# Attention feeding two mixtures of experts on one core: for pairs 13 to 23, q and k turned by 32x32 block transposes on VectorE

## The chip, the core and the metric

The kernel runs on one core of one Trainium2 chip. The metric is the device time of one execution in microseconds; three runs of the kernel before stand behind its median. A profile of one execution, taken by the hardware profiler, gives the rows shown below. Engines are PE (TensorE), DVE (VectorE), ACT (ScalarE), POOL (GpSimd) and SP (SyncE, which here only issues DMAs); PEld is TensorE's loading of weights, which overlaps its matmuls.

## What is computed

The reference, cut to what matters (all in float32; the mixtures' weights come as float64):

```python
# q, k, v: (4 batches, 12 heads, 448 rows, 64 columns)
scores = where(mask, -1e9, (1 / sqrt(64)) * q @ k.T)       # causal mask
scores = scores - max(scores, -1)
attn = exp(scores); attn = attn / (sum(attn, -1) + 1e-9)
x = (attn @ v) as (1792 tokens, 768)                        # heads side by side
h = x @ w_in                                                # w_in (768, 2048)
x = maximum(0.01 * h, h) @ w_out                            # w_out (2048, 768)
logits = x @ phi                                            # phi (768, 32): 8 experts, 4 slots each
d = softmax of logits over the tokens;  slot_input = d.T @ x
slot_out[e] = maximum(slot_input[e] @ w1[e], 0) @ w2[e]     # w1 (8, 768, 1024), w2 (8, 1024, 768)
output = (softmax of logits over the slots) @ slot_out
```

## The kernel before

**Attention.** Two heads side by side fill 128 partitions, so there are 24 pairs, six to a batch; pair n is (b, hp) = divmod(n, 6). The 448 rows are four tiles of 112 (CP). For a pair, load_qk brings q and k in with rows on partitions (tile qk, [112, 2, 512], two buffers) by four DMAs, one for q and one for k of each head; qk_stacks turns them with eight transposes on PE into PSUM tiles qkps, from which ACT casts the rounded part and DVE subtracts the remainder (tile qkt, tag qs, two buffers), so that scores are summed from parts at higher precision. The maxima of scores come from matmuls S and a custom DVE operation (junk, mxe), turned on PE (mps) and written by ACT (mr). T holds the scores less the maxima, P = exp(T) on ACT; POOL's affine_select puts zeros above the diagonal, and POOL sums P's tiles into tsum by three adds (L441, then L445 twice, over 448 and 224 elements). O = P by v, and dn, the sum by a matmul of ones with P and tsum, are on PE; rs is dn's reciprocal, O is scaled by rs and by v's scale s_v, and goes as a rounded part and a remainder to x.

**Slots.** attention_slots is a generator, three slots to an iteration n. In its second loop (n from 7 to 24, from about 104 us) slot 1 holds the last maxima of n+1, attend and inverses of n-1 and lowering of n; slot 2 T_0 and S_3; slot 3 T_1, T_2, S_0 and S_2, qk_stacks(n+2), load_qk(n+4), load_v(n+6), columns(n-1) and reduce_v(n+5). v_scale(n // 6), the scale of a batch's v, is in slot 2 of iterations 7, 13 and 19; it is a matmul v_ps on PE and five small steps on DVE that end with v_s.

**Around it.** stage() puts one slot, one unit of up(b) (18 matmuls H of w_in by x, with g = leaky relu of H on ACT and its store g_far) and steps of the weights' conversion side by side. The conversion takes raw float64 words (raw_i, raw_o) to float32: two ACT operations (cv and cs), two DVE operations on integers (L216, L217), a multiply on POOL (cv by cs), for w_in a maximum (w_am) and scale besides, and for w_out a store to wsc. One raw load waits for the last load of attention in the program, by issue_after(last_load[0]).

**Order.** All PE instructions are chained in program order (in_order), ACT's too in the later stages (fixed). DVE, POOL and SP follow a scheduler that works from priorities; attention has a raised one. Every DMA is issued by SP, in order. conv1 is the pool of the first stage (to iteration 6); gring and conv2 reuse its space tile by tile as it comes free. att, on the other side of the memory, lives to the end of attention.

Of the kernel before, what the change touches and what calls it, by code (L numbers as in the profile page):

```python
# [34 lines left out]
def tile_attn_moe_softmoe(ctx: ExitStack, tc: tile.TileContext, q, k, v, w_in, w_out, phi, w1, w2, out, dbg=None):  # L35
    nc = tc.nc
# [291 lines left out]
    def load_qk(n):  # L328
        b, hp = divmod(n, NP)
        t = att.tile([CP, 2, 2 * NI * D], F32, tag="qk", bufs=2, name=f"qk{n}")  # L330
        t = t.rearrange("p j (c x) -> p j c x", c=NI)
        for j, src in enumerate((q, k)):
            for a in range(2):
                nc.sync.dma_start(
                    t[:, j, :, D * a : D * (a + 1)], src[b, 2 * hp + a].rearrange("(c p) d -> p c d", p=CP)
                )
        qk_t[n] = t
        loaded_last()
# [25 lines left out]

    def qk_stacks(n):

        t = qk_t.pop(n)
        st = att.tile([128, 2, 2, S], F32R, tag="qs", bufs=2, name=f"qkt{n}")
# [93 lines left out]
    def inverses(n):  # L462
# [20 lines left out]
        r_t[n] = r = att.tile([128, CP], F32, tag="r", bufs=1, name=f"r{n}")  # L483
# [27 lines left out]
    NPAIR = B * NP  # L511
    onesr = att.tile([128, CP], F32R, name="onesr")
# [4 lines left out]
    for m in (0, 64):  # L517
# [3 lines left out]
    first = att.tile([128, NI, 2, 64], F32, name="first")  # L521
    nc.gpsimd.memset(first, 0.0)
    nc.gpsimd.affine_select(
        out=first, in_=first, compare_op=ALU.not_equal, fill=1.0, base=0, pattern=[[-16, NI], [-64, 2], [0, 64]],
        channel_multiplier=1,
    )
    sixteen = att.tile([128, NI, 64], F32, name="sixteen")
    nc.gpsimd.memset(sixteen, 0.0)
    for i in range(NI):
        nc.gpsimd.memset(sixteen[:, i, 16 * i : 16 * i + 16], 1.0)  # L530
# [10 lines left out]
    def attention_slots():  # L541
# [11 lines left out]
        for n in range(NP + 1):  # L553
# [27 lines left out]
            if n + NP < NPAIR:  # L581
                load_v(n + NP)
            if NP <= n + NP - 1 < NPAIR:
                reduce_v(n + NP - 1)
            yield

        for n in range(NP + 1, NPAIR + 1):
# [5 lines left out]
            if here:  # L593
                lowering(n)
            yield
# [4 lines left out]
            if n % NP == 1 and n + NP - 2 < NPAIR:  # L600
                v_scale(n // NP)
# [6 lines left out]
            if n + 2 < NPAIR:  # L608
                qk_stacks(n + 2)
                if n + 4 < NPAIR:  # L610
                    load_qk(n + 4)
            if n + NP < NPAIR:
                load_v(n + NP)
            columns(n - 1)
            if n + NP - 1 < NPAIR:
                reduce_v(n + NP - 1)
# [220 lines left out]
    if True:  # L837
        pools[0] = tc.alloc_tile_pool(name="conv1", bufs=1)
        load_qk(0)
# [265 lines left out]
VRING = 7  # L1105
# [35 lines left out]
```

## Time and profile before

| | us |
|---|---|
| median of 3 runs | 659.64 |
| lowest, highest | 658.25, 660.18 |
| the profiled execution | 656.54 |
| its span, first to last instruction | 654.8 |
| PE busy in the span | 589.6 (90%) |
| DVE busy | 366.3 (56%) |
| ACT busy | 291.1 (44%) |
| POOL busy | 235.5 (36%) |

A page of the profile has the busy time of each engine and the chain of work that ended last, followed back from the last instruction to what released it at each step. A timeline has one engine's instructions by start, with the idle time before each and, behind an arrow, what ended it. A wait is put down to what came last. An engine that idles off the chain costs nothing.

### The profile page before, as it was taken

What the parts mean: (1) busy time and instruction counts of PE and PEld (TensorE: products, weight loads), DVE (VectorE), ACT (ScalarE), POOL (GpSimd) and SP (SyncE); (2) the same over time, 40 slices, a digit from 0 to 9 for tenths busy, and PEclk for the clock granted to TensorE, in tenths of its full rate; (3) what the DMA queues carried; (4) which work ended last, traced back from release to release, by engine and by line L of the source; (5) the groups of instructions that cost most, each with busy time, mean ns of one, the idle gap of its engine ahead of it and who ended that gap; (6) DMA issues with size and microseconds to landing.
All of it is one profiled execution on the core that took longest, in us unless ns stands there. A gap on an engine that the chain in (4) does not pass through costs nothing.

```text
span 654.8 us, 12495 instructions
## 1 busy us (share of the span) xinstructions
PE 589.6 (90%) x4938; PEld 341.8 (52%) x4938; DVE 366.3 (56%) x884; ACT 291.1 (44%) x571; POOL 235.5 (36%) x247
## 2 busy tenths in 40 slices
PE   3678888998999999999999999999989999998794
PEld 2455555655555565665556555554434444553454
DVE  5868658989956665747457766533674332001014
ACT  2577556678864556755546554431212111011013
POOL 5187963489584445525335532430000000000000
PEclk9999989998999999999999999999999998899997
DMA  9942336764542466553335323029967439999958
GB/s 180 283 122 50 72 75 187 212 181 135 156 134 71 132 201 193 169 158 99 83 105 135 80 68 97 29 67 334 397 238 293 162 143 381 427 419 422 425 227 336
DMA packets 102594, 125.69 MB, mean 192 GB/s; under 512 B 69256, under 2 KB 91272, under 8 KB 98440
## 3 DMA queue, kind: packets, MB, share of 16 engines
q1 hardware_dynamic: 102536, 124.89, 58.3%
q8 instruction: 39, 0.64, 0.4%
q14 instruction: 19, 0.16, 0.1%
HBM read 105.74 MB, written 19.14 MB: 191 GB/s over the span
## 4 chain that ended last, share of the span: by engine, by line
PE 62%; DMA 11%; DVE 9%; POOL 8%; ACT 5%; issue 3%; SPq 1%; ACTq 0%; POOLq 0%; DVEq 0%
PE H L102 28%; DMA w<-in_moe_w_dram 8%; PE O L102 5%; PE T L102 5%; PE g_acc L102 3%; PE S L102 3%; PE dn L102 2%; DVE g_nat L635 2%; PE qkps L102 2%; DMA raw_i_None<-in_moe_w_in_dram 2%; PE L L102 2%; PE wt_ps L102 2%; PE ph L989 2%; POOL w L245 2%; ACT P L113 2%
## 5 line engine op out<-in xcount | busy, mean ns | idle before, releaser
L102 PE MATMUL H<-x,w 128*128 128x448 f16 x1152 | 230.9, 355 | 0.7 <-ACT g L113 0.7
L102 PEld LDWEIGHTS <-w 128*128 128x128 f16 x1152 | 111.2, 99 | 111.8 <-issue 19.0
L396 DVE CUSTOM_DVE_ANT_0 junk<-S,mask 112x224 bf16<-112x224 f32 (+3 forms) x192 | 85.2, 444 | 59.9 <-PE S L102 57.0
L474 DVE RECIPROCAL rs<-rs 128x224 f32<-128x224 f32 x36 | 53.4, 1523 | 40.3 <-ACT rs L113 40.3
L113 ACT ACTIVATE P<-T 112x672 f32<-112x672 f32 (+1 forms) x72 | 57.0, 793 | 22.2 <-PE T L102 21.0
L436 POOL TENSOR_SCALAR_AFFINE_SELECT P<-P 112x448 f32<-112x448 f32 x48 | 31.0, 648 | 91.0 <-ACT P L113 53.8
L102 PE MATMUL T<-qkt 64*112 64x336 f32 (+3 forms) x576 | 60.1, 321 | 4.1 <-ACT P L113 3.3
L113 ACT ACTIVATE g<-H,iv 128x448 f32<-128x448 f32 x48 | 30.4, 634 | 66.6 <-PE H L102 47.4
L102 PE MATMUL O<-P,v 112*64 112x448 f32 (+3 forms) x384 | 52.5, 414 | 4.5 <-POOL P L436 4.4
L102 PEld LDWEIGHTS T<-qkt 64*112 64x112 f32 x576 | 42.7, 179 | 14.3 <-issue 5.7
L445 POOL TENSOR_TENSOR tsum<-tsum,P 112x448 f32<-112x448 f32 (+1 forms) x48 | 47.3, 986 | 1.9
L102 PEld LDWEIGHTS O<-P,v 112*64 112x64 f32 x384 | 25.4, 139 | 29.4 <-issue 11.9
L441 POOL TENSOR_TENSOR tsum<-P 112x672 f32<-112x672 f32 x24 | 39.1, 1629 | 1.8
L113 ACT ACTIVATE g_spare<-H,iv 128x448 f32<-128x448 f32 x16 | 10.1, 634 | 66.5 <-PE H L102 66.5
L102 PE MATMUL S<-qkt 64*112 64x224 f32 (+3 forms) x192 | 31.9, 373 | 8.5 <-DVE mxe L396 3.7
L981 POOL MEMSET hz<- 128x256 f32 x2 | 0.6, 311 | 104.1 <-PE g_acc L102 104.1
L374 DVE TENSOR_TENSOR qkt<-qkps,qkt 128x448 fp32r<-128x448 f32 x48 | 29.1, 621 | 9.8 <-ACT qkt L113 9.8
L102 PE MATMUL T<-mr,onesr 64*112 64x448 f32 (+1 forms) x192 | 30.7, 316 | 3.9 <-ACT mr L113 3.9
L236 POOL TENSOR_TENSOR cv_i_None<-cv_i_None,cs_i_None 128x768 f32<-128x768 f32 x16 | 28.6, 1786 | 12.0 <-ACT cs_i_None L113 12.0
L113 ACT ACTIVATE mr<-mps,own 128x112 fp32r<-128x112 f32 x96 | 26.2, 360 | 14.9 <-PE mps L102 14.8
L113 ACT COPY rs<-dn 128x448 f32<-128x448 f32 x18 | 9.6, 532 | 50.3 <-PE dn L102 50.3
L254 POOL TENSOR_TENSOR cv_o_None<-cv_o_None,cs_o_None 128x768 f32<-128x768 f32 x10 | 16.5, 1646 | 42.4 <-DVE cv_o_None L217 18.4
(178 smaller groups left out, 920.9 us busy)
## 6 DMA issues: line engine op xcount, KB each, us to landing
w<-in_moe_w_dram SPq DMA_DIRECT2D x31, 1536.0 KB
raw_i_None<-in_moe_w_in_dram SPq DMA_DIRECT2D x16, 768.0 KB
raw_o_None<-in_moe_w_out_dram SPq DMA_DIRECT2D x10, 768.0 KB
g_far<-g SPq DMA_DIRECT2D x32, 224.0 KB
gb<-g_far SPq DMA_DIRECT2D x8, 896.0 KB
wo<-wsc SPq DMA_DIRECT2D x4, 1536.0 KB
qk<-in_q_dram SPq DMA_DIRECT2D x48, 112.0 KB
qk<-in_k_dram SPq DMA_DIRECT2D x48, 112.0 KB
```

Source lines behind the costliest of these rows:

```text
L102: op(*args, **kwargs)
L113: op(*args, **kwargs)
L236: nc.gpsimd.tensor_tensor(t, t, sg, ALU.mult)
L245: nc.gpsimd.tensor_tensor(lo, w, hi, ALU.subtract)
L254: nc.gpsimd.tensor_tensor(wo, wo, sg, ALU.mult)
L374: nc.vector.tensor_tensor(st[:, j, 1], p, st[:, j, 0].bitcast(F32), ALU.subtract)
L396: nc.vector.tensor_tensor_reduce(out=junk[:, :w], in0=ps[:, a, at : at + w], in1=mask[:, S - w :], scale=-1.0, scalar=3e38, op0=ALU.add, o ...
L436: nc.gpsimd.affine_select(out=d, in_=d, compare_op=ALU.is_ge, fill=0.0, base=0, pattern=[[0, 4], [1, CP]], channel_multiplier=-1,)
L441: nc.gpsimd.tensor_tensor(tsum[:CP], p[0][:CP, :, 0, CP:], p[0][:CP, :, 1, : S - CP], ALU.add)
L445: nc.gpsimd.tensor_tensor(y, y, p[1][:CP, :, j, : S - CP * (j + 2)], ALU.add)
L474: nc.vector.reciprocal(rs[:, c : c + S // 2], rs[:, c : c + S // 2])
L635: nc.vector.transpose(g_nat[:, :, 32 * f : 32 * (f + n)].rearrange("p c (f x) -> p f c x", x=32), gts[b, f].rearrange("p (c x) -> p c x", ...
```

## The change

For pairs from BLOCKS = 13 on, load_qk brings each head's q and k in with eight DMAs of 32 partitions by 14 runs of 32 elements (128 bytes a run), in such a way that two 32x32 block transposes on DVE (qk_turn) give q and k with the 64 columns of two heads on the 128 partitions. The results (qx, two buffers) are in SBUF, and ACT's cast and DVE's subtract read them there; the eight PE transposes of the pair are gone. qk_turn(n+2) is in slot 1 and qk_stacks(n+2) in slot 2 for these pairs. In the second loop load_qk(n+4) stands in slot 1, and each load from pair 9 on is put right behind SP's last instruction in the program. qk tiles of the first nine pairs are in conv1, as are first, sixteen and r; qs has three buffers. load_v and reduce_v come one pair later, the ring of v has six buffers in place of seven, and v_scale is in slot 3 ahead of columns. The diff, without moves of the constants first and sixteen:

```diff
--- before.py
+++ after.py
@@ -327,13 +327,27 @@
 
     def load_qk(n):
         b, hp = divmod(n, NP)
-        t = att.tile([CP, 2, 2 * NI * D], F32, tag="qk", bufs=2, name=f"qk{n}")
+        behind = last_on(mybir.EngineType.SP) if n >= NP + 3 else None
+        if n >= BLOCKS:
+            t = att.tile([128, 2, 2 * NI * D], F32, tag="qk", bufs=2, name=f"qk{n}")[:, :, :S]
+            for j, src in enumerate((q, k)):
+                for a in range(2):
+                    rows = src[b, 2 * hp + a].rearrange("(c i) (e x) -> e i c x", i=32, x=32)
+                    for e in range(2):
+                        o = 64 * a + 32 * e
+                        with tc.issue_after(behind):
+                            nc.sync.dma_start(t[o : o + 32, j].rearrange("i (c x) -> i c x", x=32), rows[e])
+            qk_t[n] = t
+            loaded_last()
+            return
+        t = (pools[0] if n < NP + 3 else att).tile([CP, 2, 2 * NI * D], F32, tag="qk", bufs=2, name=f"qk{n}")
         t = t.rearrange("p j (c x) -> p j c x", c=NI)
         for j, src in enumerate((q, k)):
             for a in range(2):
-                nc.sync.dma_start(
-                    t[:, j, :, D * a : D * (a + 1)], src[b, 2 * hp + a].rearrange("(c p) d -> p c d", p=CP)
-                )
+                with tc.issue_after(behind) if behind is not None else ExitStack():
+                    nc.sync.dma_start(
+                        t[:, j, :, D * a : D * (a + 1)], src[b, 2 * hp + a].rearrange("(c p) d -> p c d", p=CP)
+                    )
         qk_t[n] = t
         loaded_last()
 
@@ -362,10 +376,27 @@
         nc.vector.tensor_reduce(am[:, NP:], am[:, :NP], AX.X, ALU.max)
         s_v[b], inv_v[b] = pow2_scale(am[:, NP:], f"v{b}")
 
+    turned = {}
+
+    def qk_turn(n):
+
+        if n < BLOCKS:
+            return
+        t = qk_t.pop(n)
+        turned[n] = xs = [att.tile([128, S], F32, tag="qx", bufs=2, name=f"qx{n}_{j}") for j in range(2)]
+        for j, x in enumerate(xs):
+            nc.vector.transpose(x.rearrange("p (c x) -> p c x", x=32), t[:, j].rearrange("p (c x) -> p c x", x=32))
+
     def qk_stacks(n):
 
+        st = att.tile([128, 2, 2, S], F32R, tag="qs", bufs=3, name=f"qkt{n}")
+        if n >= BLOCKS:
+            for j, x in enumerate(turned.pop(n)):
+                scalar.copy(st[:, j, 0], x)
+                nc.vector.tensor_tensor(st[:, j, 1], x, st[:, j, 0].bitcast(F32), ALU.subtract)
+            st_t[n] = st
+            return
         t = qk_t.pop(n)
-        st = att.tile([128, 2, 2, S], F32R, tag="qs", bufs=2, name=f"qkt{n}")
         for j in range(2):
             p = ps_tr(f"qkps{n}_{j}", (128, S))
             for c in range(NI):
@@ -480,7 +511,7 @@
                 mm(
                     dn[64 * a : 64 * a + 64], sixteen[:, i], x, start=i == 0, stop=i == NI - 1, skip_group_check=True,
                 )
-        r_t[n] = r = att.tile([128, CP], F32, tag="r", bufs=1, name=f"r{n}")
+        r_t[n] = r = pools[0].tile([128, CP], F32, tag="r", bufs=1, name=f"r{n}")
         nc.vector.reciprocal(r, dn)
 
     def columns(n):
@@ -509,6 +540,7 @@
         nc.gpsimd.tensor_tensor(x16[b][:, hp, 1], rs, hi, ALU.subtract)
 
     NPAIR = B * NP
+    BLOCKS = 2 * NP + 1
     onesr = att.tile([128, CP], F32R, name="onesr")
     nc.vector.tensor_copy(onesr, istack[:, 0:1].to_broadcast([128, CP]))
     nc.vector.tensor_scalar(onesr, onesr.bitcast(F32), 0.0, 1.0, ALU.mult, ALU.add)
@@ -578,10 +600,10 @@
                 qk_stacks(n + 2)
                 if n + 4 < NPAIR:
                     load_qk(n + 4)
-            if n + NP < NPAIR:
-                load_v(n + NP)
-            if NP <= n + NP - 1 < NPAIR:
-                reduce_v(n + NP - 1)
+            if n > 0:
+                load_v(n + NP - 1)
+            if n > 1:
+                reduce_v(n + NP - 2)
             yield
 
         for n in range(NP + 1, NPAIR + 1):
@@ -592,28 +614,32 @@
             inverses(n - 1)
             if here:
                 lowering(n)
+            if n + 2 < NPAIR:
+                qk_turn(n + 2)
+                if n + 4 < NPAIR:
+                    load_qk(n + 4)
             yield
             if here:
                 weights(n, 0)
             if more:
                 maxima(n + 1, TILES[0])
-            if n % NP == 1 and n + NP - 2 < NPAIR:
-                v_scale(n // NP)
+            if BLOCKS <= n + 2 < NPAIR:
+                qk_stacks(n + 2)
+            if n + NP - 2 < NPAIR:
+                reduce_v(n + NP - 2)
             yield
             if here:
                 weights(n, 1)
                 weights(n, 2)
             if more:
                 maxima(n + 1, TILES[1])
-            if n + 2 < NPAIR:
+            if n + NP - 1 < NPAIR:
+                load_v(n + NP - 1)
+            if n % NP == 1 and n + NP - 2 < NPAIR:
+                v_scale(n // NP)
+            if n + 2 < BLOCKS:
                 qk_stacks(n + 2)
-                if n + 4 < NPAIR:
-                    load_qk(n + 4)
-            if n + NP < NPAIR:
-                load_v(n + NP)
             columns(n - 1)
-            if n + NP - 1 < NPAIR:
-                reduce_v(n + NP - 1)
             yield
 
     TILES = ((3,), (0, 2), (1,))
@@ -1102,7 +1138,7 @@
 MIX = ""
 NSPARE = 6
 GAP = 5
-VRING = 7
+VRING = 6
 GAPS = (6, 15)
 
 
```

**VectorE, iterations 9 and 10** (S10 are score tiles of pair 10, qkt11 pair 11, cv_i13 a block of w_in, S11_1 the first maxima of iteration 10). Before:

```order
L396 ISA junk10_2_1_1992,mxe0_142<-S10_0_1981,mask_114 112x336
L396 ISA mxe0_142 112x1
L374 TENSOR_TENSOR qkt11_1994<-qkps11_0_1995,qkt11_1994 128x448
L374 TENSOR_TENSOR qkt11_1994<-qkps11_1_2002,qkt11_1994 128x448
L215 TENSOR_REDUCE w_am13_2022<-cv_i13_None_2023 128x1
L216 TENSOR_SCALAR cv_i13_None_2023<-cv_i13_None_2023 128x768
L217 SCALAR_TENSOR_TENSOR cv_i13_None_2023<-raw_i13_None_1694,cv_i13_None_2023 128x768
L129 TENSOR_REDUCE w12_m1_2057<-w12_ps_2055 128x1
L396 ISA junk11_1_0_2068,mxe1_143<-S11_1_2065,mask_114 112x224
```

Now:

```order
L405 TENSOR_TENSOR qkt11_2003<-qkps11_0_2004,qkt11_2003 128x448
L427 ISA junk10_2_1_1999,mxe0_131<-S10_0_1988,mask_114 112x336
L427 ISA mxe0_131 112x1
L405 TENSOR_TENSOR qkt11_2003<-qkps11_1_2011,qkt11_2003 128x448
L215 TENSOR_REDUCE w_am13_2023<-cv_i13_None_2024 128x1
L388 STREAM_TRANSPOSE qx13_0_2352<-qk13_1867 128x448
L216 TENSOR_SCALAR cv_i13_None_2024<-cv_i13_None_2024 128x768
L217 SCALAR_TENSOR_TENSOR cv_i13_None_2024<-raw_i13_None_1697,cv_i13_None_2024 128x768
L388 STREAM_TRANSPOSE qx13_1_2353<-qk13_1867 128x448
L129 TENSOR_REDUCE w12_m1_2058<-w12_ps_2056 128x1
L427 ISA junk11_1_0_2069,mxe1_132<-S11_1_2066,mask_114 112x224
```

Pair 13's two transposes have come in around the two integer steps of cv_i13, ahead of the maxima S11_1.

**GpSimd, iterations 13 and 14** (P0 and tsum are pair 14, x16 of rs13 pair 13, cv_o4 and cv_o5 blocks of w_out). Before:

```order
L436 AFFINE_SELECT P0_448_144<-P0_448_144 112x4x112
L441 TENSOR_TENSOR tsum_148<-P0_448_144 112x672
L436 AFFINE_SELECT P0_224_145<-P0_224_145 112x4x112
L445 TENSOR_TENSOR tsum_148<-tsum_148,P0_224_145 112x2x224
L509 TENSOR_TENSOR x16_2_2887<-rs13_2967,x16_2_2887 128x448
L445 TENSOR_TENSOR tsum_148<-tsum_148,P0_224_145 112x2x112
L254 TENSOR_TENSOR cv_o4_None_3156<-cv_o4_None_3156,cs_o4_None_3157 128x768
L254 TENSOR_TENSOR cv_o5_None_3271<-cv_o5_None_3271,cs_o5_None_3272 128x768
```

Now:

```order
L467 AFFINE_SELECT P0_448_133<-P0_448_133 112x4x112
L472 TENSOR_TENSOR tsum_137<-P0_448_133 112x672
L467 AFFINE_SELECT P0_224_134<-P0_224_134 112x4x112
L540 TENSOR_TENSOR x16_2_2887<-rs13_2964,x16_2_2887 128x448
L476 TENSOR_TENSOR tsum_137<-tsum_137,P0_224_134 112x2x224
L254 TENSOR_TENSOR cv_o4_None_3153<-cv_o4_None_3153,cs_o4_None_3154 128x768
L476 TENSOR_TENSOR tsum_137<-tsum_137,P0_224_134 112x2x112
L254 TENSOR_TENSOR cv_o5_None_3287<-cv_o5_None_3287,cs_o5_None_3288 128x768
```

The first of the two conversions, cv_o4, has moved from behind the last sum to ahead of it; the same stands for pairs 15 and 16.

**ScalarE, iteration 13, slot 3** (P1 is pair 13, x16 of rs12 is pair 12, which takes the new scale of v; wp_ps and wt_ps are PSUM tiles of the mixture that share two buffers with qkps and v_ps). Before:

```order
L113 ACTIVATE P1_448_146<-T13_1_2819 112x2x336
L113 ACTIVATE P1_224_147<-T13_2_2831 112x2x336
L113 CAST qkt15_2865<-qkps15_0_2866 128x448
L113 CAST qkt15_2865<-qkps15_1_2873 128x448
L113 CAST x16_2_2887<-rs12_2703 128x448
L113 ACTIVATE cv_o2_None_2894<-raw_o2_None_2171 128x768
L113 ACTIVATE cs_o2_None_2895<-raw_o2_None_2171 128x768
L113 ACTIVATE g1_2_2923<-H1_2_2904,iv1_2724 128x448
L113 COPY w4_0_2933<-wp_ps0_2926 96x128
L113 COPY wt1_2935<-wt_ps1_0_2936 128x384
L113 COPY wt1_2935<-wt_ps1_1_2941 128x384
```

Now:

```order
L113 ACTIVATE P1_448_135<-T13_1_2828 112x2x336
L113 ACTIVATE P1_224_136<-T13_2_2840 112x2x336
L113 CAST x16_2_2887<-rs12_2704 128x448
L113 ACTIVATE cv_o2_None_2891<-raw_o2_None_2182 128x768
L113 ACTIVATE cs_o2_None_2892<-raw_o2_None_2182 128x768
L113 ACTIVATE g1_2_2920<-H1_2_2901,iv1_2738 128x448
L113 COPY w4_0_2930<-wp_ps0_2923 96x128
L113 COPY wt1_2932<-wt_ps1_0_2933 128x384
L113 COPY wt1_2932<-wt_ps1_1_2938 128x384
```

The casts of qkt15 have left slot 3 (they stand a slot ahead, behind P of T13_0); x16 now follows the P of this pair. On TensorE v_ps has moved from behind S_3 in slot 2 to behind S_0 and S_2 in slot 3, where qkps was.

## Rows read from the trace of the kernel before

**Rows 1.** The page: the chain that ended last, by engine and by line.

```profile
PE 62%; DMA 11%; DVE 9%; POOL 8%; ACT 5%; issue 3%; SPq 1%; ACTq 0%; POOLq 0%; DVEq 0%
PE H L102 28%; DMA w<-in_moe_w_dram 8%; PE O L102 5%; PE T L102 5%; PE g_acc L102 3%; PE S L102 3%; PE dn L102 2%; DVE g_nat L635 2%; PE qkps L102 2%; DMA raw_i_None<-in_moe_w_in_dram 2%; PE L L102 2%; PE wt_ps L102 2%; PE ph L989 2%; POOL w L245 2%; ACT P L113 2%
```

**Rows 2.** Busy time by stretch: window, length, busy per engine, clock.

```profile
164.00:182.00 18.00, 16.86 (x124) 10.08 (x120) 17.80 (x43) 14.74 (x26) 11.11 (x9) 1.00 0.51 154
...
182.00:395.00 213.00, 207.60 (x1610) 124.39 (x1612) 132.71 (x306) 121.44 (x253) 101.17 (x93) 1.00 0.44 124
```

**Rows 3.** Waits of PE, 182 to 395 us: total, times, longest.

```profile
PE wt_ps L102 <- ACT wprime L113: 1.9, 6, 0.7
```

**Rows 4.** Pieces of the chain of waits: start, length, what.

```profile
196.18 0.92 PE qkps L102 x8
...
389.13 0.92 PE qkps L102 x8
```

**Rows 5.** By tile: durations in ns, minimum, median, maximum; first and last start.

```profile
L102 PE MATMUL qkps<-ident,qk x192: 259/259/451, 4.1 to 389.8; 112*128 112x112 f32 x192
...
L374 DVE TENSOR_TENSOR qkt<-qkps,qkt x48: 611/620/626, 5.7 to 391.2; 128x448 fp32r<-128x448 f32 x48
...
L635 DVE STREAM_TRANSPOSE g_nat<-g x16: 631/645/647, 343.3 to 445.0; 128x448 f32<-128x448 f32 x16
```

**Rows 6.** Waits of DVE, 182 to 395 us.

```profile
DVE junk L396 <- PE S L102: 44.5, 23, 6.1
```

**Rows 7.** Timelines at iterations 9 and 10: DVE, PE, SP.

```profile
161.94 2.86 DVE L216 TENSOR_SCALAR cv_i_None<-cv_i_None 128x768 int32<-128x768 int32 x1
...
166.04 0.32 PE L102 MATMUL mps<-ident,mxe 112*128 112x112 f32 x1 [0.58 <-DVE w_m L129]
...
158.41 1.03 SPq L334 DMA_DIRECT2D qk<-in_q_dram  x2
```

**Rows 8.** Timelines around tsum: POOL and PE, then DVE beside them.

```profile
257.30 1.37 POOL L445 TENSOR_TENSOR tsum<-tsum,P 112x224 f32<-112x224 f32 x1
...
260.49 0.73 PE L102 MATMUL dn<-tsum,onesr 128*64 128x336 f32 x4
...
298.69 1.37 POOL L445 TENSOR_TENSOR tsum<-tsum,P 112x224 f32<-112x224 f32 x1
...
301.25 0.73 PE L102 MATMUL dn<-tsum,onesr 128*64 128x336 f32 x4
...
415.85 0.66 POOL L445 TENSOR_TENSOR tsum<-tsum,P 112x224 f32<-112x224 f32 x1
...
416.56 0.79 PE L102 MATMUL dn<-tsum,onesr 128*64 128x336 f32 x4 [0.19 <-POOL tsum L445]
...
248.30 0.96 DVE L217 SCALAR_TENSOR_TENSOR cv_o_None<-raw_o_None,cv_o_None 128x768 int32<-128x768 int32 x1
...
256.48 1.67 DVE L217 SCALAR_TENSOR_TENSOR cv_o_None<-raw_o_None,cv_o_None 128x768 int32<-128x768 int32 x1
```

**Rows 9.** DMA packets, 197 to 200 and 25.5 to 26.5; SP's waits.

```profile
DMA packets 1387, 0.34 MB, mean 115 GB/s; under 512 B 1387, under 2 KB 1387, under 8 KB 1387
...
DMA packets 1031, 0.21 MB, mean 206 GB/s; under 512 B 1005, under 2 KB 1031, under 8 KB 1031
...
SPq L699 <- ACT g L113: 54.6, 15, 9.2
```

**Rows 10.** Timelines of iteration 13: PE, DVE, ACT.

```profile
223.96 0.49 PE L102 MATMUL v_ps<-ident,v_am 128*128 128x128 f32 x2
...
227.52 0.68 DVE L507 SCALAR_TENSOR_TENSOR rs<-O,v_s,rs 128x448 f32<-128x448 f32 x1
...
231.20 0.97 ACT L113 CAST qkt<-qkps 128x448 fp32r<-128x448 f32 x2 [0.36 <-PE qkps L102]
232.05 0.58 ACT L113 CAST x<-rs 128x448 f16<-128x448 f32 x1
```

**Rows 11.** ACT's waits, 0 to 60 us.

```profile
30.37 0.93 ACT L113 ACTIVATE cv_i_None<-raw_i_None 128x768 f32<-128x768 f32 x1 [2.95 <-DMA raw_i_None<-in_moe_w_in_dram]
```

More of the change, by code (lines that the diff above doesn't have):

```diff
@@ L520, in tile_attn_moe_softmoe @@
         )
[L521 to L530, printed above, removed]
     mxe = [att.tile([CP, 128], F32, name=f"mxe{x}") for x in range(2)]
@@ L838, in tile_attn_moe_softmoe @@
         pools[0] = tc.alloc_tile_pool(name="conv1", bufs=1)
+        first = pools[0].tile([128, NI, 2, 64], F32, name="first")
+        nc.gpsimd.memset(first, 0.0)
+        nc.gpsimd.affine_select(
+            out=first, in_=first, compare_op=ALU.not_equal, fill=1.0, base=0, pattern=[[-16, NI], [-64, 2], [0, 64]],
+            channel_multiplier=1,
+        )
+        sixteen = pools[0].tile([128, NI, 64], F32, name="sixteen")
+        nc.gpsimd.memset(sixteen, 0.0)
+        for i in range(NI):
+            nc.gpsimd.memset(sixteen[:, i, 16 * i : 16 * i + 16], 1.0)
         load_qk(0)
```

## The prediction

> **What bounds the kernel now.** First the page's engine totals (TensorE is busy in 90% of the span) and the chain that ended last [rows 1]: TensorE holds 62% of it; the transposes by matmul that the change takes away (`qkps`) hold 2%. Then busy time by stretch [rows 2]: from 182 to 395 us, where ten of the eleven changed pairs lie (the eleventh transposes at 389.1), TensorE is busy for 207.6 of 213 us at full clock, VectorE for 133. So there a microsecond off TensorE is a microsecond off the end, until another engine is late. Which one is late next is told by TensorE's waits there [rows 3]: the longest group is 1.9 us in six waits for ScalarE; none is for VectorE's maxima or GpSimd's sums. From 164 to 182 us it is otherwise: VectorE is busy for 17.8 of 18 us and is itself the chain. Near the end the load of the last weights (`w`, 8% of the span) is on the chain [rows 1]; it is released by work that the change leaves as it is, so I carry a shift at 395 us on to the end one to one.
>
> **What is taken from TensorE.** A pair's eight transposes stand on the chain as one piece of 0.92 us, between the S matmuls and the next H; there are eleven such pieces, from 196.18 to 389.13, of which the first and the last are shown [rows 4]. The single matmul shows 259 ns [rows 5], so eight would be 2.1 us; I take the chain's 0.92, since they overlap and the next H starts right after it. The order shows that only those 22 rows, of four transposes each, leave TensorE. **11 x 0.92 = 10.1 us, a gain.**
>
> **What VectorE and ScalarE get.** Two block transposes of 128x448 f32 a pair: the trace has this shape, 645 ns [rows 5]; 22 x 0.645 = 14.2 us. The two casts (0.97 us together [rows 10]) and the two subtracts (620 ns each [rows 5]) stay and move a slot ahead. From 182 to 395 us VectorE waits 44.5 us for S matmuls [rows 6], some 4 us a pair, against 1.3 us added: hidden by that wait, and 14.2 us dear if that cover were gone. ScalarE's casts stand in slot 2 behind the P of T_0, where H takes 3.41 us and the work ahead of the next g (casts 0.97, conversions 1.8) takes 2.8: hidden, with 0.6 us to spare. One thing changes in kind: the subtract read PSUM and now reads two SBUF tiles. Before, it never took over 626 ns [rows 5]; the conversion that reads two SBUF tiles (L217) took 0.96 us with GpSimd idle and 1.67 beside GpSimd's sums, which themselves took 1.37 beside it and 0.66 without [rows 8]. So a subtract can now cost 0.6 to 1.3 us. I count nothing for it, as slot 2 has VectorE's wait, but it feeds the second rival. The Trainium skill ("SBUF — State Buffer", Who interferes with whom) says that a VectorE instruction with two SBUF inputs and a GpSimd instruction that reads SBUF exclude each other through a shared port; the rows just named agree, and if all 22 subtracts doubled VectorE would get 14 us more, by that page, against none in my sum.
>
> **The first turn, iteration 10: a loss of 2.0 us (1.3 to 3.5).** The order puts pair 13's two transposes between the conversion steps of cv_i13, into the stretch where VectorE is the chain: ahead of a step of 2.86 us at 161.94, some rows before the maxima that mps reads, for which TensorE waited 0.58 us already [rows 7]. So both transposes count, 1.3 us. The load: its buffer comes free with pair 11's transposes on TensorE (158.2), and then come eight issues. Two issues took 1.03 us from 158.41 [rows 7], so four of the eight, all that the first transpose needs, are out at about 160.5. A pair's 448 KB in 256-byte packets moves at 1387 packets in some 2.6 us [rows 9], which at 128 bytes would be 3584 packets in 6.7 us at the same packet rate; the stretch that comes nearest to 128-byte packets has 1031 in a microsecond [rows 9], so 3.5 us. I take the latter, as it is the nearest in kind: half of it takes 1.75, and the last of its packets land some 2 us after the fourth issue, at 162.6, 0.7 us after the transpose's place at 161.9. 1.3 + 0.7 = 2.0; with the slower rate 3.5, with none 1.3. Later turns come nearly two iterations after their buffer is free, of 19.3 us each in the mean (389.13 - 196.18 over ten [rows 4]).
>
> **v's scale a slot later: a loss of 2.5 us (1.0 to 4.5).** In iteration 13, v_ps was on TensorE at 223.96, rs, which needs v's scale, ran from 227.52, and ScalarE's x cast of it at 232.05, late only by its place in line [rows 10]. Now v_ps stands where qkps stood (the casts of qkps began at 231.20 [rows 10]), is done at about 231.0, and its five steps lie between S_0's junks on VectorE, done at about 233.4; rs 0.68 more: 234.1. ScalarE waits there in order with x, and behind it are cv_o and cs_o (0.9 each), g and the copy of wp_ps. x 0.5, cv and cs 1.7, g 0.6, copy 0.25: 237.2. The second wt_ps on TensorE takes the PSUM buffer that this copy frees, and would be due at 235.45 - 0.92 + 0.5, near 235.0. **2.0 us (1 to 3)**. Iterations 7 and 19 have the same step with no raw_o conversion of this size behind it: 0.5 for the two (0 to 1.5).
>
> **GpSimd's order: a loss of 1.7 us (0.6 to 2.7).** For pairs 14, 15 and 16 a cv_o add of 1.65 us is put ahead of the last tsum, which dn on TensorE waits for. Before, pair 14's last tsum ended at 258.67 and dn<-tsum began at 260.49: 1.8 us to spare, of which 0.92 goes with qkps; the order takes 1.65: late by 0.7 at most, by nothing if the last tsum runs in 0.66. Pair 15 shows the same 1.8. Pair 16: end 300.06, dn 301.25, so late by 0.7 to 1.4 [rows 8]. Central values 0.4, 0.4, 0.9. For the other eight pairs the order keeps the sums together or puts in half an add. What they then do is seen in pair 23, which has no qkps ahead of it and an add of 0.92 in between: dn waited 0.19 us [rows 8]. 8 x 0.1 = **0.8 us (0 to 1.6)**.
>
> **The start: a gain of 0.5 us (-1.3 to +1.0, the gain cut to 1.0 as other waits follow).** One v load of 224 KB fewer is issued ahead of the raw weights; by the 2.6 us of 448 KB [rows 9] raw_i comes up to 1.3 us earlier, and ScalarE waited 2.95 us for one [rows 11]. Against it GpSimd's first pair has an add of 1.8 us moved ahead of its select. The later weights' buffers (raw_i6 on) now wait for pair 8's transposes on TensorE, in iteration 6; the conversions that read them are an iteration later, and I count nothing, but a late one would cost its lateness once.
>
> **Sum.** 10.1 + 0.5 - 2.0 - 2.5 - 1.7 - 0.8 = 3.6 us. The profiled run had a span of 654.8 and a time of 656.54, which becomes 652.9; the median of the runs is 3.1 us above that run, 659.64, and I predict against the median: **656.0**. With every bound at its best the gain is 8.2 (651.4), at its worst a loss of 3.5 (663.1).
>
> **Rivals.** (1) *All covers hold*: no loss at all, 659.64 - 10.1 = 649.5. For it: VectorE's 44.5 us of waiting and TensorE's few waits. Against it: iteration 10 and iteration 13 have their losers on the chain or a row behind it.
> (2) *The wait takes the place of the transposes*: dn waits for the sums in every pair. Pair 14's sums had 1.8 us to spare [rows 8], less 0.92; contention with the subtracts, or an x cast 0.9 us later, in each pair eats the rest. Then 8 x 0.7 more is lost, 3.6 - 5.6 = -2.0, which is 661.6; half of it gives 658.8, and that I take for this case: no change.
> (3) *Slower: the loads come late to an in-order VectorE.* A turn stands ahead of S_0's junks, so a late load holds the maxima, mps, mr and T. SP issues in order, and its waits for g reach 9.2 us [rows 9]; with eight issues (4.1) and 6.7 us of packets that is 20 us, a whole iteration. It decides from the point where a load lands over two iterations after its release or, for SP, where qk stands behind a g that waits in each; if six turns are late by 2 us, 3.6 - 12 = -8.4: 668; if three, 662. Against it: the loads have nearly two. The Trainium skill ("DMA: Bandwidth & Descriptors", Bandwidth, and Why small descriptors are slow (HBM only)) speaks against this edit: transfers under 64 KB are dominated by descriptors, and a load here becomes 56 KB in 128-byte runs; by its fixed cost of three cycles a packet the bytes would cost (4+3)/4 against (8+3)/8, an estimated 27% more, so some 3.3 us for the 2.6, which alone does not make this rival. No row of before has a stretch of 128-byte packets alone.
> That the edit does not do what it says is excluded: the 22 rows of four transposes are gone from TensorE's order.
>
> **How the numbers follow.** About 0.3%, 2 us, is what a measurement of this kernel can tell from no change. Forecast (a gain of 2 to 7): 0.40. Rival 1 (more than 7): 0.14. Rival 2 (within 2): 0.25. Slower, by rival 3 or by the upper bounds of my losses together: 0.21. Faster 0.54, same 0.25, slower 0.21. The range runs from 649.5 to 662: it leaves out some 0.04 below and the worse half of the slower cases, 0.11, above.
>
> **What would show it.** In the changed kernel's trace: TensorE's chain without qkps from 182 us on, S followed by H (the gain); VectorE idle ahead of the transposes of pair 13 and mps late by 2 us at about 166 (first turn); wt_ps waiting for a ScalarE copy near 235 (v's scale); dn waiting for tsum in pairs 14 to 16 and by not more than 0.2 in others (GpSimd). If dn waits by 0.5 or more in most pairs, rival 2 is right; if VectorE idles ahead of turns past pair 13, rival 3. The prediction is wrong above all if the end from 440 us on does not carry the shift.

## The result, and the profile after

The changed kernel takes 661.9 us, the median of 11 runs (659.95 to 665.99); the kernel before took 657.88 in 11 runs beside it and earlier (655.53 to 660.18). The ratio is 1.0069, with a 95% interval of 1.0046 to 1.0092: slower, by about 4 us. The profiled execution has a span of 659.1 us against 654.8. From its page, the first line and the busy time of the engines:

```profile
span 659.1 us, 12407 instructions
...
PE 586.9 (89%) x4850; PEld 334.3 (51%) x4850; DVE 369.5 (56%) x906; ACT 290.5 (44%) x571; POOL 235.0 (36%) x247
```

TensorE is busy for 2.7 us less, in a span that is 4.3 us longer. So the matmuls did go, and more than their time came back as waiting and as a lower clock. What TensorE waits for, from 100 to 400 us of the changed kernel (who waits, for what, total, times, longest; [rows 3] has the same view of the kernel before, from 182 us on):

```profile
PE dn L102 <- POOL tsum L476: 6.1, 6, 2.0
PE S L102 <- ACT P L113: 2.7, 1, 2.7
...
PE T L102 <- DVE mxe L427: 1.2, 1, 1.2
...
PE qkps L102 <- DVE v_am L369: 0.9, 1, 0.9
```

In the same window of the kernel before, the first and the last group are missing, and the one for mxe is

```profile
PE T L102 <- DVE mxe L396: 0.5, 1, 0.5
```

Where the span went is seen best by cutting it at the first matmul of O of a pair (iteration n runs from the O of pair n-1 to that of pair n; lengths in us, from the timelines of TensorE; e1 to e3 are the first three experiments below):

| stretch | before | after | e1_sums | e2_hold | e3_both |
|---|---|---|---|---|---|
| start to O of pair 6 | 104.2 | 102.0 | 107.1 | 101.7 | 102.1 |
| iteration 7 | 18.64 | 25.05 | 22.98 | 18.82 | 18.83 |
| 8 to 10 | 59.79 | 59.49 | 58.67 | 59.55 | 58.67 |
| 11 and 12 | 33.68 | 35.40 | 31.97 | 35.38 | 31.97 |
| 13 and 14 | 42.05 | 41.49 | 41.45 | 41.41 | 41.41 |
| 15 to 17 | 62.25 | 64.44 | 60.50 | 65.35 | 60.76 |
| 18 to 23 | 112.76 | 109.65 | 109.11 | 109.59 | 109.11 |
| O of pair 23 to the end | 221.4 | 221.6 | 220.1 | 219.9 | 220.8 |

Two places lose: **iteration 7**, 6.4 us, where no pair is turned yet, and **iterations 11, 12 and 15 to 17**, where the gain of the turned pairs has become a loss of 3.9. From iteration 18 on the gain is there, and the end carries the shift one to one.

**Iteration 7.** VectorE there (start, length, what, and in brackets the idle time before it and what ended it):

```profile
111.64 0.69 DVE L371 TENSOR_REDUCE v_am<-v 112x1 f32<-112x512 f32 x1 [3.13 <-DMA v<-in_v_dram]
...
115.11 0.62 DVE L427 CUSTOM_DVE_ANT_0 junk<-S,mask 112x448 bf16<-112x448 f32 x1
```

SP's issues in the same timeline, ahead of it:

```profile
100.62 1.56 SPq L183 DMA_DIRECT2D raw_i_None<-in_moe_w_in_dram  x3
104.16 0.33 SPq L357 DMA_DIRECT2D v<-in_v_dram  x1
```

VectorE stands for 3.13 us in front of the maximum of v for pair 12, the first of the third batch. With six buffers v of pair 12 has to wait for O of pair 6 (which starts at 102.02); SP issues it at 104.16, after three loads of raw weights, and it lands at about 111.6. The program writes this maximum in iteration 8, and holds each maximum behind VectorE's last instruction of the program at that point. For the first pair of a batch, though, reduce_v clears the batch's tile first, so that the last instruction is that clearing: an instruction that has nothing to wait for but the tile, and which the scheduler may put early. That of pair 12's batch ran at 18.88 us. So nothing held the maximum at its place in the program any more; the scheduler put it into iteration 7, ahead of its own data, and everything behind it on VectorE is 3 us late. The kernel before has the same hold: there the ring of seven let v of pair 12 be issued at 94.30, and the maximum ran at 130.65 without a wait. A ring of seven in the changed kernel was not tried. On TensorE:

```profile
115.79 0.57 PE L102 MATMUL T<-qkt 64*112 64x224 f32 x6 [1.20 <-DVE mxe L427]
...
118.40 1.01 PE L102 MATMUL qkps<-ident,qk 112*128 112x112 f32 x4 [0.60 <-DVE w_m L129]
120.34 1.01 PE L102 MATMUL qkps<-ident,qk 112*128 112x112 f32 x4 [0.93 <-DVE v_am L369]
121.14 5.49 PE L102 MATMUL H<-x,w 128*128 128x448 f16 x18
```

TensorE waits by pieces, 1.20, 0.60 and 0.93 us (and 0.20 for v_ps), and then its 18 matmuls H take 5.49 us where they take 3.57 in most other places. The busy time by stretch has the reason (window, length, busy per engine in the order of the page, then the granted clock, the share of the DMA engines and GB/s):

```profile
116.00:120.00 4.00, 2.60 (x26) 1.83 (x24) 3.93 (x13) 1.26 (x2) 3.83 (x4) 0.77 0.00 0
120.00:124.00 4.00, 3.66 (x12) 1.99 (x13) 3.30 (x17) 1.19 (x3) 1.06 (x3) 0.50 0.33 74
124.00:128.00 4.00, 4.00 (x21) 2.06 (x21) 1.12 (x4) 2.30 (x4) 1.01 (x1) 0.87 0.97 270
```

A granted clock of 0.50 is the lower of the two levels, 1.2 GHz. The waits cost 2.9 us, H 1.9 more, and the transposes ahead of it are slow as well.

**The sums.** GpSimd at pair 15:

```profile
283.66 1.14 POOL L476 TENSOR_TENSOR tsum<-tsum,P 112x448 f32<-112x448 f32 x1
284.75 1.64 POOL L254 TENSOR_TENSOR cv_o_None<-cv_o_None,cs_o_None 128x768 f32<-128x768 f32 x1
286.35 0.65 POOL L476 TENSOR_TENSOR tsum<-tsum,P 112x224 f32<-112x224 f32 x1
```

and TensorE beside it:

```profile
284.68 0.36 PE L102 MATMUL dn<-P,onesr 128*64 128x112 f32 x4
287.05 0.79 PE L102 MATMUL dn<-tsum,onesr 128*64 128x336 f32 x4 [2.01 <-POOL tsum L476]
...
287.92 3.57 PE L102 MATMUL H<-x,w 128*128 128x448 f16 x18
```

The conversion's product stands between the last two sums, as the order had it, and dn waits 2.01 us for the last; the granted clock stayed at 1.00 there (284 to 292 us), and the next H took 3.57. Pairs 14 and 16 wait 1.02 and 0.98. At pair 11 the remainder of w takes that place, in front of both sums; GpSimd:

```profile
204.34 1.65 POOL L245 TENSOR_TENSOR w<-cv_i_None,w 128x768 f16<-128x768 f32 x1
205.94 1.87 POOL L476 TENSOR_TENSOR tsum<-tsum,P 112x448 f32<-112x448 f32 x2
```

and TensorE:

```profile
207.86 0.79 PE L102 MATMUL dn<-tsum,onesr 128*64 128x336 f32 x4 [1.30 <-POOL tsum L476]
...
211.35 4.75 PE L102 MATMUL H<-x,w 128*128 128x448 f16 x18
```

Here H is slow again, 4.75 us, after the wait of 1.30 and one of 0.64 for mr.

### The profile page after: what moved, and what is told of

Its sections match the earlier page's. It is cut to its first block, busy times and chain, and to the rows that moved or that the text cites. A ratio compares the mean times of both kernels' runs of the same rounds, so it can differ in the third digit from the quotient of the medians.

```text
span 659.1 us, 12407 instructions
## 1 busy us (share of the span) xinstructions
PE 586.9 (89%) x4850; PEld 334.3 (51%) x4850; DVE 369.5 (56%) x906; ACT 290.5 (44%) x571; POOL 235.0 (36%) x247
## 4 chain that ended last, share of the span: by engine, by line
PE 37%; DMA 8%; DVE 4%; ACT 1%; POOL 1%; issue 0%; POOLq 0%; DVEq 0%; ACTq 0%; SPq 0%
PE H L102 18%; DMA w<-in_moe_w_dram 8%; PE g_acc L102 3%; DVE g_nat L661 2%; PE T L102 2%; PE L L102 2%; PE O L102 2%; PE ph L1025 2%; PE o L1096 1%; PE psi L997 1%; PE dn L102 1%; PE wt_ps L102 1%; PE S L102 1%; ACT P L113 1%; PE pgt L102 1%; PE lt L102 0%
## 5 line engine op out<-in xcount | busy, mean ns | idle before, releaser
L102 PE MATMUL H<-x,w 128*128 128x448 f16 x1152 | 235.7, 360 | 0.7 <-ACT g L113 0.7
L476 POOL TENSOR_TENSOR tsum<-tsum,P 112x448 f32<-112x448 f32 (+1 forms) x48 | 44.4, 924 | 1.5
L472 POOL TENSOR_TENSOR tsum<-P 112x672 f32<-112x672 f32 x24 | 40.5, 1689 | 1.7
L236 POOL TENSOR_TENSOR cv_i_None<-cv_i_None,cs_i_None 128x768 f32<-128x768 f32 x16 | 27.1, 1695 | 17.7 <-ACT cs_i_None L113 17.7
L540 POOL TENSOR_TENSOR x<-rs,x 128x448 f16<-128x448 f32 x24 | 28.8, 1199 | 10.5 <-ACT x L113 10.5
```

The lines of the kernel that those rows point to most:

```text
L102: op(*args, **kwargs)
L236: nc.gpsimd.tensor_tensor(t, t, sg, ALU.mult)
L472: nc.gpsimd.tensor_tensor(tsum[:CP], p[0][:CP, :, 0, CP:], p[0][:CP, :, 1, : S - CP], ALU.add)
L476: nc.gpsimd.tensor_tensor(y, y, p[1][:CP, :, j, : S - CP * (j + 2)], ALU.add)
L540: nc.gpsimd.tensor_tensor(x16[b][:, hp, 1], rs, hi, ALU.subtract)
```

## The experiments

Theory: two faults of order, neither of them in the turns, cost what the turns bring: (A) the maximum of v for pair 12 is ordered ahead of its data; (B) conversion work on GpSimd stands ahead of the sums that dn waits for. Rivals: the turns themselves do not pay (VectorE's added work, late loads or contention cost what TensorE saves). A third suspect is v's scale in slot 3. Four of the kernels change the order alone, four how many pairs are turned. e1_sums, e2_hold, e3_both and e4_noturn were timed beside the kernel before at 657.64 us, the others beside it at 657.34.

**e1_sums: the sums first.** In the changed kernel, GpSimd's product of cv_o and the remainder of w (the latter in the later stages only) are held behind the last add of tsum that precedes them in the program (last_sum is set behind the adds in weights):

```diff
-        nc.gpsimd.tensor_tensor(lo, w, hi, ALU.subtract)
+        with tc.issue_after(last_sum[0]) if fixed[0] and last_sum[0] is not None else ExitStack():
+            nc.gpsimd.tensor_tensor(lo, w, hi, ALU.subtract)
...
-            nc.gpsimd.tensor_tensor(wo, wo, sg, ALU.mult)
+            with tc.issue_after(last_sum[0]) if last_sum[0] is not None else ExitStack():
+                nc.gpsimd.tensor_tensor(wo, wo, sg, ALU.mult)
...
+            last_sum[0] = last_on(mybir.EngineType.Pool)
```

> The changed kernel with one thing put back: on GpSimd each conversion multiply (cv_o) and each w_in remainder is ordered behind the last tsum add of the newest pair; no other engine's order changes. Theory 1 (GpSimd's order took the place of the transposes): TensorE's waits of dn for tsum, 6.1 us in the changed kernel (1.30, 1.02, 2.01, 0.98 and two of 0.38), fall under 0.5, the H at 211 us that took 4.75 us after such a wait goes back to 3.5, and the time falls by 5 to 7 us, to 655 to 657. Theory 2 (only iteration 7 matters): the waits go, but something behind them is late by as much, and the time stays within 2 us of 661.9. Rival 3 of the prediction (late loads): no change.

Measured: 652.33 us (10 runs), ratio 0.9924 [0.9896, 0.9953]. Waits of dn for the sums fall from 6.1 to 0.5 us. In the table, iterations 11 and 12 and 15 to 17 shrink by 3.4 and 3.9 us, iterations 8 to 10 by 0.8; iteration 7 still has 4.1 more than e3_both. VectorE, ScalarE and SP run their instructions in the same order as in the changed kernel; only GpSimd's differs. So B is 9.6 us of medians (661.9 - 652.3).

**e2_hold: the maximum stays in its place.** What the maximum is held behind is looked up ahead of the clearing:

```diff
+        ahead = last_on(mybir.EngineType.DVE) if b else None
         if hp == 0:
             v_am[b] = am = const.tile([128, NP + 1], F32, tag="v_am", bufs=2, name=f"v_am{b}")
             nc.vector.memset(am, 0.0)
-        with tc.issue_after(last_on(mybir.EngineType.DVE)) if b else ExitStack():
+        with tc.issue_after(ahead) if b else ExitStack():
```

> The changed kernel with one thing put back: the first maximum of a batch's v (pairs 12 and 18) is held at its place in the program, where in the changed kernel only the clearing of its tile ahead of it was; on VectorE it moves from iteration 7 to iteration 8, nothing else does. Theory 2 (VectorE waits in order for v of pair 12, which lands behind three raw loads): VectorE's wait of 3.1 us at 108.5 goes, TensorE's waits in iteration 7 (1.2, 0.2, 0.6, 0.9) and its fall to the lower clock with them, iteration 7 falls from 25.0 us to 19 to 20, and the time by 5 to 6.5 us, to 655.5 to 657. If raw loads that come late on ScalarE, or v's scale a slot later, are the cause instead, iteration 7 stays over 23 us and the time over 660.

Measured: 654.52 us (10 runs), 0.9965 [0.9941, 0.9988]. On VectorE the maxima of pairs 6, 12 and 18, the first of their batches, move, and one step of the conversion beside that of pair 12 changes its place. Pair 6's move shows in no time: O of pair 6 starts at 101.69 us, against 102.02. Iteration 7 takes 18.82 us, about as before the change (18.64), and the waits for the sums remain (6.0 us). A is 7.4 us (661.9 - 654.5).

**e3_both: both edits.**

> Both orders put back, GpSimd's multiplies behind the sums and the first maxima of v in their place; the transposes on VectorE stay. If the two are the whole loss and add up, the time is 661.9 - 6 - 6 = 650 (648.5 to 652), about 1.2% under the kernel before. If one hides the other, or a third wait follows (wt_ps for ScalarE in iteration 13, mr for T), it stays at 653 to 656. If late loads or transposes on VectorE are the cause, over 658.

Measured: 646.06 us (4 runs, 645.04 to 649.13), 0.9843 [0.9796, 0.9891]: the fastest version, 1.6% faster than the kernel before and 2.4% faster than the change. Its page:

```profile
span 643.6 us, 12414 instructions
```

and its waits of TensorE from 100 to 400 us:

```profile
PE S L102 <- ACT P L114: 2.7, 1, 2.7
...
PE dn L102 <- POOL tsum L480: 0.5, 1, 0.5
```

The sums now come one behind the other and the product follows, as these rows of GpSimd at pair 15 show:

```profile
272.13 1.87 POOL L480 TENSOR_TENSOR tsum<-tsum,P 112x448 f32<-112x448 f32 x2
273.96 1.64 POOL L257 TENSOR_TENSOR cv_o_None<-cv_o_None,cs_o_None 128x768 f32<-128x768 f32 x1
```

In the stretch where the change lost its clock, that of e3_both stays whole (busy time by stretch):

```profile
116.00:120.00 4.00, 4.00 (x26) 2.33 (x25) 3.31 (x15) 1.64 (x4) 3.76 (x4) 1.00 0.35 79
120.00:124.00 4.00, 4.00 (x33) 2.25 (x31) 3.30 (x10) 2.57 (x5) 1.03 (x1) 1.00 1.01 291
```

A and B together are 15.8 us. They add up nearly: 7.4 and 8.5 one way (e2, then e3), 9.6 and 6.3 the other. By the ratios to the kernel before, together they are 14.9.

**e4_noturn and e5_both_noturn: no pair turned**, in the changed kernel and in e3_both. TensorE transposes all pairs again; the rest of the change (buffers of v, slots, loads in order) stays.

```diff
-    BLOCKS = 2 * NP + 1
+    BLOCKS = 4 * NP
```

> The changed kernel with TensorE's transposes for all pairs (no block transposes, loads of q and k by four DMAs, qk_stacks in slot 3 again); v later, six v buffers, the pools and load_qk in slot 1 stay. If the block transposes save what the chain said (10.1 us, of which dn's waits for the sums give back some 3.6 as each gets 0.92 more room), the time is 666 to 670. If the transposes on VectorE or their loads are what made the change slow, it is under 660.

> The kernel with both orders put back (646.06 us), but with TensorE's transposes for all pairs, as in the run without block transposes. This prices the block transposes with the two waits gone. If they are worth what the chain of waits showed, 11 x 0.92 = 10.1 us, less 1.3 for the first turn: 655 to 656. If dn's wait for the sums hides part of it even now: 650 to 653. If they are worth only the 2.6 us by which the earlier pair of runs differed (664.5 against 661.9): 648 to 649.

Measured: e4_noturn 664.48 us (4 runs), 1.0140 [1.0074, 1.0205]; e5_both_noturn 655.35 (10 runs), 0.9969 [0.9937, 1.0001]. With both orders mended the turns are worth 655.35 - 646.06 = 9.3 us (8.3 by their ratios to the kernel before). In the order of the change they are worth 664.48 - 661.9 = 2.6 (4.7 by the ratios, whose intervals overlap: from four runs of e4_noturn, this is not clear of noise). In e4_noturn dn waits for the sums, from 100 to 400 us:

```profile
PE dn L102 <- POOL tsum L476: 0.7, 2, 0.4
```

In the change it is 6.1: nearly all waits of B come with the turns. These take 0.92 us of TensorE's work from ahead of dn, and GpSimd's order is another; which of the two weighs more was not separated. The wait of iteration 7 is in e4_noturn too (25.5 us between the two O, from 102.5 to 128.0); it has nothing to do with the turns.

**e6_vslot2: v's scale back in slot 2**, in e3_both.

```diff
@@ slot 2
+            if n % NP == 1 and n + NP - 2 < NPAIR:
+                v_scale(n // NP)
@@ slot 3
-            if n % NP == 1 and n + NP - 2 < NPAIR:
-                v_scale(n // NP)
```

> The kernel with both orders put back, and v's scale in slot 2 again in place of slot 3. The prediction put the later scale at 2.5 us; the traces show one wait of 0.89 to 0.97 us of wt_ps for ScalarE in iteration 13. By the trace: that wait goes and the time is 645 (644 to 646.5). By the prediction's term: 643.5. If the scale in slot 2 holds VectorE up elsewhere: 647 or more.

Measured: 666.25 us (4 runs), 1.0106 [1.0033, 1.0178]. The expectation missed by some 20 us. The waits of TensorE from 100 to 400 us:

```profile
PE v_ps L102 <- DVE v_am L380: 14.0, 3, 5.3
```

and a piece of iteration 13, TensorE:

```profile
228.79 0.77 PE L102 MATMUL v_ps<-ident,v_am 128*128 128x128 f32 x2 [5.32 <-DVE v_am L380]
229.36 5.28 PE L102 MATMUL H<-x,w 128*128 128x448 f16 x18
```

with VectorE's last maximum of v ahead of it:

```profile
226.39 0.67 DVE L375 TENSOR_REDUCE v_am<-v 112x1 f32<-112x512 f32 x1
```

The last maximum of a batch is now made in slot 2 of the same iteration, at 226.39, since loads and maxima of v come a pair later; with the scale in slot 2, v_ps comes up on TensorE before that maximum is made and waits 4.06, 5.32 and 4.60 us, and H after each takes 5.25 to 5.55. So the later slot is no cost that could have been left out; it goes with the later maxima, and in slot 3 v_ps waited 0.20 us in the changed kernel.

**e8_blocks9 and e9_blocks15: more pairs turned, and fewer**, in e3_both: from pair 9 on, or from pair 15 on.

```diff
-    BLOCKS = 2 * NP + 1
+    BLOCKS = NP + 3
```

and for e9_blocks15:

```diff
-    BLOCKS = 2 * NP + 1
+    BLOCKS = 2 * NP + 3
```

> The kernel with both orders put back, with pairs 9 to 12 turned on VectorE too (15 pairs in place of 11); their transposes leave TensorE in iterations 7 to 10. If VectorE is the bound there, as its busy time of 17.8 of 18 us from 164 to 182 said, each of them costs up to 1.3 us and saves nothing in iterations 9 and 10: 647 to 650. If TensorE's time counts there too: 646 - 3.7 = 642.4.

> The kernel with both orders put back, with pairs 13 and 14 on TensorE again (9 pairs turned). By the prediction's term for the first turn (2.0 us lost on VectorE in iteration 10, 0.92 saved on TensorE) leaving pair 13 out gains 1.1 and leaving pair 14 out loses 0.9: 645.9. If the first turn costs nothing on the chain, as its trace shows no wait for a load: 646 + 1.8 = 647.9.

Measured: e9_blocks15 648.91 us (4 runs), 0.9841 [0.9796, 0.9887], not told apart from e3_both; the spans are 644.8 and 643.6. Two pairs on TensorE cost about 1.2 us there by the spans, so turning pairs 13 and 14 brings little, and costs nothing. e8_blocks9: 656.29 us (10 runs), 0.9976 [0.9946, 1.0005], 10 us slower than e3_both for four pairs more. From the O of pair 7 to that of pair 10 (busy time by stretch):

```profile
123.37:185.00 61.63, 53.25 (x357) 30.73 (x359) 60.52 (x124) 47.49 (x83) 41.63 (x31) 0.94 0.62 161
```

The waits of TensorE from 100 to 400 us:

```profile
PE S L102 <- ACT P L114: 4.6, 3, 2.5
PE dn L102 <- POOL tsum L480: 3.6, 3, 1.6
PE mps L102 <- DVE w_m L130: 2.6, 3, 1.9
```

And by tile the subtract from 120 to 200 us (ns, minimum, median, maximum):

```profile
L400 DVE TENSOR_TENSOR qkt<-qx,qkt x8: 617/1696/2066, 134.4 to 196.4; 128x448 fp32r<-128x448 f32 x8
```

VectorE is busy for 60.5 of 61.6 us (in e3_both 54.1 of 58.7 between the same two O): it is the bound there, and TensorE waits for it and for what hangs on it. These iterations hold 2.7 of the 8.0 us between the two spans; iteration 7 has 1.0, 11 and 12 have 2.2, and the rest lies in the start and the end. And the subtract, 620 ns in the changed kernel, has a median of 1696 ns. It stands beside GpSimd's work; VectorE, two in a row:

```profile
134.39 3.55 DVE L400 TENSOR_TENSOR qkt<-qx,qkt 128x448 fp32r<-128x448 f32 x2
```

GpSimd at the same time:

```profile
133.81 1.65 POOL L247 TENSOR_TENSOR w<-cv_i_None,w 128x768 f16<-128x768 f32 x1 [3.42 <-ACT w L114]
135.42 2.03 POOL L237 TENSOR_TENSOR cv_i_None<-cv_i_None,cs_i_None 128x768 f32<-128x768 f32 x1
```

In every row of e3_both and e8_blocks9 where a subtract took over 0.7 us, GpSimd ran a product or a remainder beside it; in the changed kernel GpSimd was idle during all 22. How much of e8_blocks9's loss is this, and how much the added transposes, was not separated.

## Why the prediction was right or wrong

The forecast was a gain of 3.6 us and 656.0; the kernel lost 4.0. Two steps failed: the sum had no term for the maxima of v that the edit moves (A, 6.3 to 7.4 us), and GpSimd's order was put at 2.5 us where it cost 8.5 to 9.6 (B). Put together, the 9.3 us that the turns bring and some 2 of the rest of the change (not clear of noise), less the 15.8 of A and B, leave a loss of 4.5, near the measured 4.0. Step by step:

**The bound, and what is taken from TensorE: right.** Predicted 11 x 0.92 = 10.1; measured 9.3 (8.3 by the ratios) between e5_both_noturn and e3_both. An undisturbed iteration (14 and 17 to 21 of e3_both against before) is shorter by 0.8 us rather than 0.92. VectorE's added 14.2 us were hidden by its wait for S, as said: that wait was 44.9 us from 100 to 400 us before and 33.4 after. Rival 3 did not come as described: not one transpose of the changed kernel waited for a load. The late load that did hold VectorE was one of v.

**v's scale a slot later: the step that failed most.** Its paragraph asked where v_ps and rs would stand, and for iterations 7 and 19 it took 0.5 us. Iteration 7 lost 6.4. The prediction followed the scale but not the maxima and the loads that were moved with it: "load_v and reduce_v come one pair later, the ring of v has six buffers" stood in the change, and no term of the sum held it. The order of VectorE would have shown the maximum of pair 12 ahead of instructions of iteration 7, and the code showed what it is held behind. That is A, 6.3 to 7.4 us. In iteration 13 the mechanism was the one described, with half the size, 0.97 for 2.0; ScalarE's cast:

```profile
238.90 0.56 ACT L113 CAST x<-rs 128x448 f16<-128x448 f32 x1 [2.73 <-DVE rs L538]
```

and TensorE, which waits for the copy behind it:

```profile
241.81 0.55 PE L102 MATMUL wt_ps<-ident,cv_o_None 128*128 128x128 f32 x3 [0.97 <-ACT w L113]
```

**GpSimd's order: right in kind, mis-sized.** For pairs 14 to 16 it had 0.4, 0.4 and 0.9 us; the waits were 1.02, 2.01 and 0.98, in all 4.0 for 1.7. The prediction let part of the product hide under the rest of dn; at pair 15 it began at 284.75, 0.07 us after that rest had begun, and was paid nearly whole. The other pairs were put at 0.1 each because the order "keeps the sums together or puts in half an add"; but at pair 11, whose dn follows the place where pair 13's transposes were, a whole remainder of 1.65 us stood ahead of both sums (wait 1.30). What the sum lacked altogether is the clock: waits of 1 to 3 us on TensorE were charged at their length, while H after some of them took 1.2 to 2.0 us more. B measures 8.5 to 9.6 for the 2.5 that both terms had. Rival 2 had these waits at all eleven places, by 0.7 us; they came at four of them, from 0.98 to 2.01, and twice by 0.38 at pairs 8 and 10, ahead of the first. That its full price, 661.6, is the measured time is chance: the stall of iteration 7 is no part of it.

**The first turn: a term that was not there.** The two transposes stood where the order had them, and did not wait. VectorE:

```profile
165.82 0.65 DVE L388 STREAM_TRANSPOSE qx<-qk 128x448 f32<-128x448 f32 x1
166.39 1.70 DVE L216 TENSOR_SCALAR cv_i_None<-cv_i_None 128x768 int32<-128x768 int32 x1
...
169.35 0.63 DVE L388 STREAM_TRANSPOSE qx<-qk 128x448 f32<-128x448 f32 x1
```

SP's issues of the two loads that they read:

```profile
162.16 1.89 SPq L339 DMA_DIRECT2D qk<-in_q_dram  x4
164.09 2.04 SPq L339 DMA_DIRECT2D qk<-in_k_dram  x4
```

Against the 1.3 us that they add, the step between them took 1.70 us where [rows 7] had 2.86. Where no earlier stall disturbs it, in e3_both, mps waits 1.11 us for the 0.58 of before; that 0.5 is what is left of the 2.0, and e9_blocks15, without this turn, is no faster. The first four loads were out 1.8 us, and the other four 3.2 us, before the transposes that read them.

**Contention of the subtract: counted at nothing, rightly here, and real.** In the changed kernel the three steps are (ns: minimum, median, maximum):

```profile
L388 DVE STREAM_TRANSPOSE qx<-qk x22: 600/634/645, 165.8 to 372.4; 128x448 f32<-128x448 f32 x22
L113 ACT CAST qkt<-qx x22: 556/561/568, 195.5 to 388.8; 128x448 fp32r<-128x448 f32 x22
L396 DVE TENSOR_TENSOR qkt<-qx,qkt x22: 615/620/625, 196.1 to 390.4; 128x448 fp32r<-128x448 f32 x22
```

The range given for a subtract beside GpSimd, up to 1.3 us, was too small: e8_blocks9 shows 2.07. The Trainium skill ("SBUF — State Buffer", Who interferes with whom) says that a VectorE instruction with two SBUF inputs contends with GpSimd's reads; the runs agree, 620 ns with GpSimd idle and up to 2.07 us beside it. Whoever took that rule as a reason to expect a loss here would have been wrong, since no subtract of the changed kernel met GpSimd; in e8_blocks9 five of eight were slow beside it.

**The start: not settled.** Predicted 0.5; the O of pair 6 came 2.2 us earlier. But over the single profiled executions of kernels whose work up to there is nearly the same it lies between 100.7 (e6_vslot2) and 107.1 us (e1_sums), so one pair of traces says nothing of its size. e5_both_noturn, which has every other part of the change, is 2.0 us below the kernel before with an interval that reaches 1.0001.

**The base.** The median of three runs, 659.64, was 1.8 us above that of eleven; against the latter the same sum gives 654.3. **The end** from 440 us on carried the shift, as assumed: 221.6 against 221.4 from the O of pair 23 on.

**Smaller slips in its readings.** All eleven pieces of qkps lie between 182 and 395 us, not ten. The dn that waited 0.19 us at 416.56 is pair 22's, not pair 23's. The 6.7 us for 3584 packets take the 2.6 us of a pair's 448 KB, which are 1792 packets of 256 bytes, for the 1387 that were counted by 200 us; at 2.6 us it would be 5.2. None of them changes a central value of the sum; the last one enters the upper bound of the first turn and rival 3.

## What to carry to other kernels

An instruction on an in-order engine that needs a transfer has to be held behind something that really stands at its place; held behind the instruction just before it in the code, which may be a clearing that runs early, it is as free as that one to go ahead of its data, and blocks the engine. Whoever shortens the bounding engine takes slack from every wait that was just met, so the order of the helpers is part of the edit: write down for each of them what now must be done first, and pin it. And a prediction has to follow every instruction that an edit moves, the small ones of the buffers as well, into the order of each engine; here two orders, one not followed and one mis-sized, cost 16 us, and the turns bring 9.

## What the runs showed of the hardware that was not expected

- The cost of a wait on TensorE is not its length. The 18 matmuls H take 3.57 us at full clock; after a wait of 2.17 us in the kernel before they took 4.12, after 1.20, 0.20, 0.60 and 0.93 us one after the other 5.49, after 5.32 us in e6_vslot2 5.28. After 2.01 us at pair 15 they took 3.57. The same wait of 2.73 us for P in iteration 9 was followed by 5.58 in the changed kernel (granted clock 0.50 from 160 to 164 us), by 4.06 in e1_sums and by 4.22 in e3_both. What decides whether the clock falls to the 1.2 GHz level was not tried.
- A subtract of 128x448 f32 on VectorE with both operands in SBUF took 620 ns with GpSimd idle and up to 2.07 us beside GpSimd's products, which themselves took 2.03 in place of 1.65.
- ScalarE's cast of 128x448 took 561 ns from SBUF, and 533 from PSUM in the kernel before.
- Eight loads of 56 KB in 128-byte runs, issued in 3.9 us, kept no transpose of the changed kernel waiting; in e9_blocks15 VectorE waited 1.9 and 0.6 us for them once.
